# Where zero products go on TensorE: placed by a running shortfall of array activity, and into a free PSUM bank too

## The chip, the cores and the metric

The kernel runs on one core of one Trainium2 chip. The metric is device time in microseconds (us) of one execution. The core's engines run side by side, each through its own list of instructions in order, and wait for one another on semaphores: TensorE (PE) for matmuls, ScalarE (ACT) for exponentials and gelus, VectorE (DVE) for copies out of PSUM, norms and arithmetic, GpSimd (POOL) for small odd jobs, and SyncE (SP), which issues DMAs. PSUM, where matmuls write, has eight banks of 128 x 512 numbers in f32.

## The reference

The input x has 2048 rows of 512. Two kinds of layer alternate, A, B, A, B, with the same weights both times, and each adds its output to x. Layer A is attention with 32 heads of width 16 that share one key and one value head; layer B is a mixer along the rows followed by an MLP.

```python
def _A_ref(x, wq, wk, wv, wo):          # x is layernorm(x); H = 32, Dh = 16
    q = (x @ wq).reshape(B, S, H, Dh).transpose(0, 2, 1, 3)
    k = x @ wk
    v = x @ wv
    p = _softmax(jnp.einsum("bhqd,bkd->bhqk", q, k) * (Dh ** -0.5))
    o = jnp.einsum("bhqk,bkd->bhqd", p, v)
    return o.transpose(0, 2, 1, 3).reshape(B, S, H * Dh) @ wo

def _B_ref(x, w1, w2, w3, w4):          # w3: 512 x 1792, w4: 1792 x 512
    h = _gelu(_layernorm(x) @ w1)
    # four column groups of h are shifted by 1, -1, 2, -2 rows: hs
    x1 = x + hs @ w2
    return x1 + _gelu(_layernorm(x1) @ w3) @ w4
```

The exponentials are most of the elementwise work: 2 x 32 x 2048 x 2048 of them.

## The kernel before

**Tiling.** The queries are cut into four chunks c of 512 rows, the heads into eight blocks b of four, the keys into 16 blocks kb of 128. One *group* is (layer, c, b, kb): four score matmuls (one for each head, line 730), each on a quarter of the array's rows (32*128), into four banks; four exponentials; and four value matmuls (line 824), each on a quarter of the array's columns (128*32), that add into the accumulator bank ACC (bank 5). There are 1024 groups. After the 16 groups of a block (`block_end`, lines 833 to 884) a DVE copy takes ACC out (line 849, or its siblings 837 and 845 where a block of the second layer is spilled and added later); reciprocals and small matmuls (lines 856 to 877) then divide by the softmax sums.

**Who computes the exponentials.** Score banks 0 to 2 and 3 to 4 are two slots that alternate. A *unit* (`declare_unit`, line 750) is one slot's score matmuls and one ACT exponential over its two or three banks (line 775). In the three-bank slot the third bank may go to DVE instead, which computes the exponential by integer arithmetic (lines 790 to 812). `assign` (line 930) gives DVE a pair of tiles when its backlog is short.

**Side work.** When a chunk's attention is done, `chunk_end` (line 951) declares all that follows for its rows: output projection (993), mixer (1027, 1069), MLP (1102, 1133), norms and transposes (582), and the next keys, values and queries (626, 641, 669). This runs beside the attention of later chunks, released at a pace, through the two pool banks 6 and 7. A side operation takes a free pool bank when it is placed and gives it back when its reader has ended (`Late`, `take`, `give`). The long gelus on ACT (lines 1041 and 1119) interrupt the exponentials. After the last attention unit the attention's banks are lent to the pool and the tail runs alone.

**The planner.** The order of each engine's instructions is made while the program is built, by `Plan`, which plays the run through with costs of its own. `_pick` takes from an engine's ready operations the one with the lowest priority number: 0 for score units, 2 for value groups, 4 to 10 for side work. `soon` in `_pick` keeps everything with a priority above 0 back while a score unit will be ready within 0.2 us. The planner models the TensorE clock: it counts full-array columns (`activity`) in windows of 3.4133 us, and a window with at least `WARM` x 2400 columns per us makes the next one run at 2400 columns per us, otherwise at 1200. On the chip only the order and the semaphores remain; no planned time is enforced.

**Fillers.** To keep activity up, the planner places zero products: a 128 x 128 block of zeros (NIL) times ONES, added into ACC, where it changes nothing (line 743). `debt` is the shortfall: `KEEP` x 2400 columns per us of time, less the columns placed, and never under -`CREDIT` (0.3 us). In the kernel before, a filler is asked for only when `_pick` found nothing at all for PE and `idle()` (line 139) says yes: a shortfall over zero, and no attention operation ready within `NEAR_FILL` (0.25 us). It has priority 20. `filler()` (line 735) places none while the latest block's copy, `last_copy`, has been declared but has not ended, since ACC is then being read. The copy is declared together with the last value group of its block, which is ahead of when it runs.

Of the kernel before, what the change touches and what calls it, by code (L numbers as in the profile page):

```python
# [31 lines left out]
class Plan:  # L32
# [12 lines left out]
    WARM = 0.36  # L45
    KEEP = 0.46
    CREDIT = 0.3
    LATER = 12.0
# [90 lines left out]
    def idle(self):  # L139

        if self.filler is None:
            return False
        t = self.now
        self.roll(t)
        if any(o.prio <= 2 and o.ready <= t + self.NEAR_FILL for o in self.heap["PE"]):
            return False
        return self.debt + self.KEEP * 2400.0 * (t - self.debt_at) > 0

# [56 lines left out]
    def _place(self, o, t):  # L205
# [10 lines left out]
        elif o.eng == "PE":  # L216
# [15 lines left out]
            self.debt = max(self.debt, -self.CREDIT * 2400.0)  # L232
# [19 lines left out]
    def run(self, pump):  # L252
        while True:
# [4 lines left out]
            t = heapq.heappop(self.events)  # L258
# [4 lines left out]
            while again:  # L263
                again = pump(self.now)
                for e in ENGINES:
                    if self.free_at[e] <= self.now + 1e-9:
                        o = self._pick(e, self.now)
                        if o is None and e == "PE" and self.idle():
                            self.filler()
                            o = self._pick(e, self.now)  # L270
                        if o is not None:
                            self._place(o, self.now)
                            again = True
# [85 lines left out]
def mm(n, k=1):  # L359
    return ("F", max(n, 60) * k, n * k)  # L360
# [6 lines left out]
class Kernel:  # L367
# [104 lines left out]
    def head(self):  # L472
# [17 lines left out]
        def fill(eng, ap, v, tags, dur, prio):  # L490
# [5 lines left out]
           reads=[("ID",)], writes=[("ID",)], dur=0.4, prio=-9)  # L496
# [4 lines left out]
           reads=[("ONES",)], pe=mm(512), prio=-9)  # L501
# [233 lines left out]
    def filler(self):  # L735

        dep = self.last_copy
        if dep is not None and not (dep.placed and dep.end + self.pl.MARGIN <= self.pl.now):
            return
        if self.last_fill is not None and not self.last_fill.placed:  # L740
            return
        o = self.last_fill = self.pl.op(
            "PE", lambda e: e.matmul(self.PB[:, self.ACC, :], lhsT=self.NIL, rhs=self.ONES, start=False,  # L743
                                     stop=False, skip_group_check=True),
            reads=[("ONES",)], pe=mm(512), prio=20)
        if dep is not None:
            o.preds.add(dep)
        self.nfill += 1
# [436 lines left out]
```

## Time and profile before

| | us |
|---|---|
| median of 3 runs | 1913.28 |
| lowest and highest | 1908.33 and 1926.69 |
| the profiled execution's own time | 1905.72 |
| its span, first to last instruction | 1903.9 |
| PE busy in it | 1764.9 (93%) |
| DVE busy | 1648.0 (87%) |
| ACT busy | 1683.7 (88%) |
| mean granted TensorE clock | 0.855 |
| fillers (line 743) | 547 |

How to read it: the page gives busy time for each engine, then the span in 40 slices with the busy share in tenths, and under PEclk the TensorE clock that the throttle granted, in tenths of full speed. Its groups name a line, an engine, an operation, the tiles out<-in, the shape, and the count, then busy time and mean ns, then the engine's idle time before them and who ended it. The trace also answers for any stretch of time (`from:to`): length, then the busy time and the number of instructions of each engine, then the granted clock, the DMA share and GB/s. Asked for one line, it gives that line's instructions alone. In order of time a row is: start, duration, engine, line, operation, count of merged instructions, and in brackets the idle time before it and what ended it. Matmuls are pipelined and their ends are modelled, so a row's duration holds some latency; the distance between two starts is the better measure of what one occupies.

### The profile page before, as it was taken

To read this page: it belongs to the slowest core of one execution; us is meant where nothing else is said; L and a number is where in the kernel's file an instruction comes from. 1 tells how busy PE (TensorE), PEld (TensorE's weight loads), DVE (VectorE), ACT (ScalarE), POOL (GpSimd) and SP (SyncE) were. 2 spreads that over 40 slices of the span, in tenths; PEclk is the share of its full clock that TensorE was granted. 3 is DMA by queue.
4 is the path that set the end of the run, shared out by engine and by line. 5 is a ranking of instruction groups with operands and counts; after the bars stand their busy time and mean duration, and the time that the engine had idled before them with its cause. 6 is when DMAs were issued, how large, how long until landed. Compare 5 with 4: busy or idle time off the path is not lost.

```text
span 1903.9 us, 32587 instructions
## 1 busy us (share of the span) xinstructions
PE 1764.9 (93%) x13284; PEld 509.4 (27%) x13284; DVE 1648.0 (87%) x3209; ACT 1683.7 (88%) x1726; POOL 59.6 (3%) x117
## 2 busy tenths in 40 slices
PE   8999999999999899999889899999899998989988
PEld 3222222323222222223222222222222222222234
DVE  7988899998889999997989589878888998999942
ACT  5999999999999999996899689888988999999942
POOL 2000000000100000001000000000000000000000
PEclk9855587999799997999989779587887989995989
DMA  5000000000000000000000000000000000000000
GB/s 167 1 1 1 1 1 1 1 1 1 1 1 1 1 1 1 1 1 1 1 1 1 1 1 1 1 1 1 1 7 4 1 1 7 7 1 1 1 12 14
DMA packets 10179, 12.07 MB, mean 6 GB/s; under 512 B 1584, under 2 KB 9520, under 8 KB 10032
## 3 DMA queue, kind: packets, MB, share of 16 engines
q1 hardware_dynamic: 10032, 10.00, 1.7%
q8 instruction: 106, 1.74, 0.4%
q14 instruction: 41, 0.34, 0.1%
HBM read 7.90 MB, written 2.10 MB: 5 GB/s over the span
## 4 chain that ended last, share of the span: by engine, by line
PE 54%; ACT 36%; DVE 9%; issue 1%; DMA 0%; POOL 0%; SPq 0%
ACT EA L775 33%; PE PB L730 20%; PE PB L824 12%; PE PB L1133 5%; PE PB L743 4%; PE PB L993 3%; PE PB L1102 3%; DVE DJ L790 2%; PE PB L669 2%; ACT G L1119 2%; PE PB L1027 1%; PE PB L582 1%; DVE ED L810 1%; DVE ED L812 1%; PE PB L1069 1%; PE PB L871 1%
## 5 line engine op out<-in xcount | busy, mean ns | idle before, releaser
L775 ACT ACTIVATE EA<-PB 128x1024 bf16<-128x1024 f32 (+2 forms) x1639 | 1571.9, 1063 | 158.2 <-PE PB L730 142.3
L730 PE MATMUL PB<-QT,KT 32*128 32x512 bf16 x4096 | 738.4, 444 | 92.9 <-ACT EA L775 70.9
L790 DVE TENSOR_SCALAR DJ<-PB 128x512 uint16<-128x512 f32 x768 | 527.9, 687 | 116.2 <-PE PB L730 111.6
L824 PE MATMUL PB<-EA,VP 128*32 128x512 bf16 x3328 | 460.0, 449 | 3.9 <-ACT EA L775 3.4
L730 PEld LDWEIGHTS PB<-QT,KT 32*128 32x128 bf16 x4096 | 161.1, 93 | 667.9 <-ACT EA L775 515.2
L824 PE MATMUL PB<-ED,VP 128*32 128x512 bf16 x768 | 339.6, 450 | 0.0
L810 DVE TENSOR_TENSOR ED<-DF,ED 128x1024 bf16<-128x1024 uint16 x384 | 261.9, 682 | 2.6
L812 DVE TENSOR_TENSOR ED<-DJ,ED 128x1024 uint16<-128x1024 uint16 x384 | 262.4, 683 | 1.1
L743 PE MATMUL PB<-ONES,NIL 128*128 128x512 bf16 x547 | 185.4, 414 | 0.7 <-DVE ACCF L849 0.7
L824 PEld LDWEIGHTS PB<-EA,VP 128*32 128x32 bf16 x3328 | 102.0, 95 | 303.2 <-issue 262.0
L804 DVE TENSOR_SCALAR DF<-DJ 128x1024 uint16<-128x1024 uint16 x384 | 162.1, 422 | 3.4
L807 DVE TENSOR_SCALAR ED<-DF 128x1024 bf16<-128x1024 uint16 x384 | 161.5, 421 | 3.6
L1133 PE MATMUL PB<-W,G 128*128 128x512 bf16 x448 | 129.2, 408 | 14.0 <-ACT G L1119 13.4
L1102 PE MATMUL PB<-ZT,W 128*128 128x384 bf16 (+2 forms) x560 | 134.2, 354 | 0.9 <-DVE ZT L589 0.7
L669 PE MATMUL PB<-YT,WQ 128*32 128x512 bf16 x1024 | 77.7, 405 | 3.1 <-DVE QT L676 1.8
L993 PE MATMUL PB<-WO,OT 128*128 128x512 bf16 x256 | 72.3, 391 | 0.7 <-DVE OT L877 0.7
L743 PEld LDWEIGHTS PB<-ONES,NIL 128*128 128x128 bf16 x547 | 47.7, 100 | 94.3 <-issue 75.7
L1112 DVE CAST G<-PB 128x512 bf16<-128x512 f32 (+2 forms) x112 | 67.6, 604 | 4.2 <-PE PB L1102 4.1
L824 PEld LDWEIGHTS PB<-ED,VP 128*32 128x32 bf16 x768 | 70.7, 95 | 0.0
L558 POOL TENSOR_SCALAR SM<-MV 128x4 f32<-128x4 f32 (+3 forms) x29 | 8.5, 293 | 1569.3 <-DVE MV L543 1569.2
L1102 PEld LDWEIGHTS PB<-ZT,W 128*128 128x128 bf16 x560 | 42.3, 99 | 55.2 <-issue 32.5
L849 DVE CAST ACCF<-PB 128x512 bf16<-128x512 f32 x57 | 39.1, 686 | 19.5 <-PE PB L824 19.0
(80 smaller groups left out, 902.3 us busy)
## 6 DMA issues: line engine op xcount, KB each, us to landing
W<-in_B_w_dram SPq DMA_DIRECT2D x2, 1792.0 KB, 12.7
X<-in_A_x_dram SPq DMA_DIRECT2D x8, 256.0 KB, 6.5
out_dram<-OUTB SPq DMA_DIRECT2D x16, 128.0 KB, 1.7
W<-in_B_w_dram SPq DMA_DIRECT2D x2, 512.0 KB, 6.7
WQ<-in_A_wq_dram SPq DMA_DIRECT2D x1, 512.0 KB, 5.9
WO<-in_A_wo_dram SPq DMA_DIRECT2D x4, 128.0 KB, 2.8
WK<-in_A_wk_dram SPq DMA_DIRECT2D x1, 16.0 KB, 6.7
WV<-in_A_wv_dram SPq DMA_DIRECT2D x1, 16.0 KB, 6.1
```

The lines of the kernel that those rows point to most:

```text
L730: return e.matmul(self.PB[:, bank, :], lhsT=self.KT[32 * h:32 * h + 32, la, kb * 128:(kb + 1) * 128], rhs=self.QT[32 * h:32 * h + 32, c % ...
L743: "PE", lambda e: e.matmul(self.PB[:, self.ACC, :], lhsT=self.NIL, rhs=self.ONES, start=False, stop=False, skip_group_check=True),
L775: o = op("ACT", lambda e: e.activation(self.EA[:, ea, 0:n, :], self.PB[:, b0:b0 + n, :], ACTF.Exp, scale=0.25), writes=[("BK", b) for b in ...
L790: o = op("DVE", lambda e: e.tensor_scalar(out=self.DJ[:, js, i * 512:(i + 1) * 512], in0=self.PB[:, bank, :], scalar1=128 * LOG2E * 0.25, ...
L804: op("DVE", lambda e: e.tensor_scalar(out=self.DF, in0=J, scalar1=0x7F, scalar2=None, op0=ALU.bitwise_and), reads=jt, writes=[("DF",)], du ...
L807: op("DVE", lambda e: e.tensor_scalar(out=E, in0=self.DF, scalar1=-129.0, scalar2=0.33 / 128, op0=ALU.add, op1=ALU.mult), reads=[("DF",)], ...
L810: op("DVE", lambda e: e.tensor_tensor(out=E, in0=self.DF, in1=E, op=ALU.mult), reads=[("DF",)], writes=et, dur=t_x2(1024), prio=2, side=Fa ...
L812: last = op("DVE", lambda e: e.tensor_tensor(out=E.bitcast(dt.uint16), in0=J, in1=E, op=ALU.add), reads=jt, writes=et, dur=t_x2(1024), pri ...
L824: ins = e.matmul(self.PB[32 * h:32 * h + 32, self.ACC, :], lhsT=self.VP[:, la, kb, :], rhs=e4[h][0], start=first, stop=(end is not None), ...
L993: ins = e.matmul(self.PB[:, L.bank, :], lhsT=self.OT[:, b, q:q + 128], rhs=self.WO[:, b, :], start=(b == 0), stop=(b == 7))
L1102: ins = e.matmul(self.PB[:, L.bank, 0:n], lhsT=self.W3[:, dc, f * 128:(f + 1) * 128], rhs=ZT[:, dc, 0:n], start=(dc == 0), stop=(dc == 3))
L1133: ins = e.matmul(self.PB[:, L.bank, :], lhsT=self.G2[:, f, i * 128:(i + 1) * 128], rhs=self.W4[:, f, :], start=(f == 0), stop=False)
```

## The change

Fillers are now considered before anything else is picked for PE. If the shortfall is over `FORCE` (0.3 us) a filler is placed even if attention is ready; if it is over zero, one is placed unless attention is ready within a look-ahead, which is `NEAR_FILL` (0.25 us) for a shortfall under `URGENT` (0.4 us) and 0 otherwise. Its priority is -20, ahead of all other work. The shortfall is held under `CAP` (0.65 us). `KEEP` goes from 0.46 to 0.53, `WARM` in the clock's model from 0.36 to 0.40. While ACC may not be touched, a filler may take a free pool bank, which it writes as a product of its own (start and stop set) and gives back at once. The first dummy matmul into ACC gets priority -30 and a tag that fillers wait for.

```diff
-    WARM = 0.36
-    KEEP = 0.46
+    WARM = 0.40
+    KEEP = 0.53
     CREDIT = 0.3
+    URGENT = 0.4
+    FORCE = 0.3
+    CAP = 0.65
...
         t = self.now
         self.roll(t)
-        if any(o.prio <= 2 and o.ready <= t + self.NEAR_FILL for o in self.heap["PE"]):
+        short = (self.debt + self.KEEP * 2400.0 * (t - self.debt_at)) / 2400.0
+        if short <= 0:
             return False
-        return self.debt + self.KEEP * 2400.0 * (t - self.debt_at) > 0
+        if short > self.FORCE:
+            return True
+        near = self.NEAR_FILL if short < self.URGENT else 0.0
+        return not any(o.prio <= 2 and o.ready <= t + near for o in self.heap["PE"])
...
-            self.debt = max(self.debt, -self.CREDIT * 2400.0)
+            self.debt = min(max(self.debt, -self.CREDIT * 2400.0), self.CAP * 2400.0)
...
+                        if e == "PE" and self.idle():
+                            self.filler()
                         o = self._pick(e, self.now)
-                        if o is None and e == "PE" and self.idle():
-                            self.filler()
-                            o = self._pick(e, self.now)
...
-           reads=[("ONES",)], pe=mm(512), prio=-9)
+           reads=[("ONES",)], writes=[("ACC0",)], pe=mm(512), prio=-30)
...
     def filler(self):
 
-        dep = self.last_copy
-        if dep is not None and not (dep.placed and dep.end + self.pl.MARGIN <= self.pl.now):
-            return
         if self.last_fill is not None and not self.last_fill.placed:
             return
+        dep = self.last_copy
+        L = None
+        if dep is not None and not (dep.placed and dep.end + self.pl.MARGIN <= self.pl.now):
+            if not any(t + self.pl.MARGIN <= self.pl.now for t, b in self.pl.pool):
+                return
+            L = Late()
         o = self.last_fill = self.pl.op(
-            "PE", lambda e: e.matmul(self.PB[:, self.ACC, :], lhsT=self.NIL, rhs=self.ONES, start=False,
-                                     stop=False, skip_group_check=True),
-            reads=[("ONES",)], pe=mm(512), prio=20)
-        if dep is not None:
+            "PE", lambda e: e.matmul(self.PB[:, self.ACC if L is None else L.bank, :], lhsT=self.NIL,
+                                     rhs=self.ONES, start=L is not None, stop=L is not None, skip_group_check=True),
+            reads=[("ONES",), ("ACC0",)], pe=mm(512), prio=-20, take=L, give=L)
+        if dep is not None and L is None:
             o.preds.add(dep)
```

## The prediction

> **What bounds the kernel now.** I read the page first.
>
> ```profile
> span 1903.9 us, 32587 instructions
> ...
> PE 1764.9 (93%) x13284; PEld 509.4 (27%) x13284; DVE 1648.0 (87%) x3209; ACT 1683.7 (88%) x1726; POOL 59.6 (3%) x117
> ...
> PEclk9855587999799997999989779587887989995989
> ...
> PE 54%; ACT 36%; DVE 9%; issue 1%; DMA 0%; POOL 0%; SPq 0%
> ...
> L775 ACT ACTIVATE EA<-PB 128x1024 bf16<-128x1024 f32 (+2 forms) x1639 | 1571.9, 1063 | 158.2 <-PE PB L730 142.3
> ...
> L730 PE MATMUL PB<-QT,KT 32*128 32x512 bf16 x4096 | 738.4, 444 | 92.9 <-ACT EA L775 70.9
> ...
> L743 PE MATMUL PB<-ONES,NIL 128*128 128x512 bf16 x547 | 185.4, 414 | 0.7 <-DVE ACCF L849 0.7
> ```
>
> ScalarE (ACT) works 1683.7 of 1903.9 us, nearly all of it in the exponentials of line 775. Of its idle time, 142.3 us ends when score matmuls of line 730 finish, so TensorE is what it waits for. TensorE has two clocks: the PEclk line dips to 5. The zero products of line 743, which I call fillers, are there 547 times. Reading the granted clock along the span, I found where it switches between 1.00 and 0.50 and asked for the busy times of stretches cut there: first the ten half-clock stretches that will turn out to begin at a block's end, then 15 full-clock ones of the main loops.
>
> ```profile
> core 0: us, PE busy (x) PEld busy (x) DVE busy (x) ACT busy (x) POOL busy (x), PEclk, DMA share, GB/s
> 77.80:251.90 174.10, 171.80 (x1017) 35.24 (x1013) 153.84 (x277) 166.84 (x170) 0.00 (x0) 0.50 0.00 1
> ...
> 1716.20:1764.00 47.80, 47.21 (x288) 10.43 (x288) 44.02 (x82) 43.37 (x46) 0.94 (x3) 0.50 0.00 1
> sum 416.40, PE 411.49 PEld 92.52 DVE 354.78 ACT 368.67 POOL 0.94; mean PE 41.15 PEld 9.25 DVE 35.48 ACT 36.87 POOL 0.09
> ```
>
> ```profile
> 306.50:497.70 191.20, 186.47 (x1516) 56.41 (x1512) 180.82 (x357) 189.23 (x197) 6.60 (x11) 1.00 0.01 1
> ...
> sum 1025.10, PE 945.48 PEld 279.63 DVE 976.88 ACT 1001.17 POOL 33.32; mean PE 63.03 PEld 18.64 DVE 65.13 ACT 66.75 POOL 2.22
> ```
>
> The next sums are, in this order, five half-clock stretches that follow a long gelu, two others, and the rest (head, change of layer, tail).
>
> ```profile
> sum 64.90, PE 59.66 PEld 11.41 DVE 37.80 ACT 47.98 POOL 0.19; mean PE 11.93 PEld 2.28 DVE 7.56 ACT 9.60 POOL 0.04
> sum 47.80, PE 46.92 PEld 10.04 DVE 37.01 ACT 38.40 POOL 0.00; mean PE 23.46 PEld 5.02 DVE 18.50 ACT 19.20 POOL 0.00
> sum 349.70, PE 301.37 PEld 115.77 DVE 241.57 ACT 227.48 POOL 25.20; mean PE 75.34 PEld 28.94 DVE 60.39 ACT 56.87 POOL 6.30
> ```
>
> At full clock ACT idles 23.9 of 1025.1 us, 2.3%. At half clock it idles 47.7 of 416.4, 16.9 of 64.9 and 9.4 of 47.8: 14% of 529 us. The other 122.2 us of idle lie in the head, the layer change and the tail, where one stage waits for the one before.
>
> What switches the clock? I cut one stretch into windows of 3.4 us, first with all matmuls, then (last two rows) with the fillers alone.
>
> ```profile
> 71.00:74.40 3.40, 2.91 (x21) 0.70 (x19) 3.19 (x7) 3.40 (x5) 0.00 (x0) 1.00 0.03 5
> 74.40:77.80 3.40, 2.36 (x22) 0.69 (x22) 3.26 (x7) 3.40 (x6) 0.00 (x0) 1.00 0.00 0
> 77.80:81.20 3.40, 2.93 (x19) 0.53 (x15) 3.40 (x7) 3.40 (x5) 0.00 (x0) 0.50 0.00 0
> 98.30:101.70 3.40, 3.40 (x19) 0.63 (x16) 2.57 (x5) 3.21 (x4) 0.00 (x0) 0.50 0.00 0
> ...
> 71.00:74.40 3.40, 1.00 (x3) 0.21 (x3) 1.00 0.03 5
> 98.30:101.70 3.40, 0.61 (x1) 0.11 (x1) 0.50 0.00 0
> ```
>
> A score (32*128) or value (128*32) matmul uses a quarter of the array for 512 columns, a filler all of it; at 2400 columns per us a window takes 8160. From 71.0 on: (18/4 + 3) x 512 = 3840, a share of 0.47, and the clock stays full. From 74.4 on: 22/4 x 512 = 2816, 0.345, and the next window is at half. At 98.3 PE is busy all the time, yet (18/4 + 1) x 512 gives 0.345 and nothing recovers. I did this for all 525 windows between 20 and 1812 us. Of 370 full-clock windows, the 336 at 0.40 or more are all followed by full clock, the 15 under 0.355 never, of the 19 between 17. Of 155 half-clock ones, none of the 82 under 0.32 is, 5 of 37 from 0.32 to 0.355, 7 of 31 from 0.355 to 0.40, 5 of 5 above. So the clock follows the amount of array work, and the limit lies near 0.37.
>
> Why the work runs out shows at the ten entries: first the copies of line 849 from 1 us before to 3 us after an entry, then the fillers in the 3.4 us before it.
>
> ```profile
> 76.80:80.80 4.00, 0.68 (x1) 0.63 0.00 0
> ...
> 1715.20:1719.20 4.00, 0.68 (x1) 0.63 0.01 2
> ...
> 74.40:77.80 3.40, 0.00 (x0) 0.00 (x0) 1.00 0.00 0
> ...
> sum 34.00, PE 0.67 PEld 0.07; mean PE 0.07 PEld 0.01
> ```
>
> Nine of the ten rows hold one such copy; the tenth entry (1118.9) has its sibling of line 845. Fillers: 0.67 us in 34. That is the rule in the old filler(): from the moment a block's copy is declared until it has ended, no filler may enter the accumulator bank. The kernel loses the clock there, and once at half it stays, since attention alone lies under the limit.
>
> **The change, part by part.** *The free pool bank* takes that gap away. If all ten stretches ran at ACT's full-clock share, 368.67 / 0.977 = 377.4 us would replace 416.4: 39 us. I take 35, since about one stretch in ten may stay. The largest is worth little: in its 174 us ACT idles only 7.3. With the 16 and 9 us of the other two sums (below) all half-clock time of the main loops is worth 63 us, 3.3% of the span. [...]
>
> *Running shortfall, KEEP 0.53, forcing.* How a filler fits shows in order of time, two ACT steps at full clock and one at half:
>
> ```profile
> 68.10 0.39 PE L730 MATMUL PB<-QT,KT 32*128 32x512 bf16 x3 [0.20 <-ACT EA L775]
> 68.42 0.40 PE L824 MATMUL PB<-EA,VP 128*32 128x512 bf16 x3
> 68.43 0.39 PE L824 MATMUL PB<-ED,VP 128*32 128x512 bf16 x1
> 69.02 0.39 PE L730 MATMUL PB<-QT,KT 32*128 32x512 bf16 x2 [0.20 <-ACT EA L775]
> 69.34 0.60 PE L743 MATMUL PB<-ONES,NIL 128*128 128x512 bf16 x2
> 69.93 0.39 PE L730 MATMUL PB<-QT,KT 32*128 32x512 bf16 x3
> ...
> 79.10 0.61 PE L730 MATMUL PB<-QT,KT 32*128 32x512 bf16 x3 [0.31 <-ACT EA L775]
> 79.64 0.61 PE L824 MATMUL PB<-EA,VP 128*32 128x512 bf16 x3
> ```
>
> At full clock three steps last 3 x 0.92 = 2.75 us and hold three score units, two value groups and two fillers. From start to start a unit takes 0.32 us; a second filler behind the first adds 0.60 - 0.39 = 0.21, so a change of kind costs about 0.11. Occupied: 5 x 0.32 + 0.53 = 2.13 of 2.75 us. Work: (16/4 + 2) x 512 = 3072 of 6600 columns, 0.465, which is the old KEEP. For 0.53 it takes 2.8 fillers, 0.8 more, which at 0.32 each need 0.26 of the 0.62 us that are free. So at full clock there is room.
>
> How many more: over all pairs of such windows from 77.8 to 1812.9 us I took today's fillers out and filled up to 0.53. That needs 872, an estimate, where the same stretch now holds 514: about 360 more. What does one cost? At least 0 where it fills a hole, at most 0.32 us where a score unit stands behind it: 0 to 115 us. A gain from them is the clock, which is counted above. The nearest rows are two stretches at full clock with many and with few fillers (first all, then fillers alone):
>
> ```profile
> 400.00:450.00 50.00, 48.93 (x352) 15.41 (x349) 42.56 (x83) 49.75 (x51) 0.00 (x0) 1.00 0.00 1
> 600.00:650.00 50.00, 44.35 (x368) 13.00 (x364) 49.78 (x97) 49.77 (x55) 0.00 (x0) 1.00 0.00 1
> ...
> 400.00:450.00 50.00, 15.39 (x56) 4.88 (x56) 1.00 0.00 1
> 600.00:650.00 50.00, 5.05 (x13) 1.24 (x13) 1.00 0.00 1
> ```
>
> With 56 fillers ACT works 49.75 of 50 us, with 13 it works 49.77: no price at all. Those stood behind the guard that looks 0.25 us ahead for attention. It stays for a shortfall up to 0.3 and is gone above, where a filler is forced. (FORCE is 0.3 and URGENT 0.4, so the branch that would drop the look-ahead to 0 is never reached.) So what the rows don't show is a forced filler ahead of a ready score unit. A filler now has priority -20 too and stands ahead of side work. I take 0.03 us, a tenth of the upper end, near the row: 11 us. The cover is ACT's 0.92 us step; where PE has no hole in it, the upper end holds.
>
> *CAP 0.65* keeps a long shortfall from being paid in one burst. Such bursts stand in the gelus, where ACT is busy for two windows:
>
> ```profile
> 1361.20:1364.70 3.50, 0.61 (x2) 0.11 (x2) 0.91 (x2) 3.48 (x3) 0.00 (x0) 0.99 0.00 0
> ...
> 1357.80:1361.20 3.40, 1.69 (x7) 0.60 (x7) 1.00 0.01 2
> ```
>
> Seven fillers run at once, then PE does two matmuls in 3.5 us, and the clock falls. On the chip nothing spaces fillers in time; they run as soon as their turn comes. So the cap cures this in part: of the 64.9 - 47.98/0.977 = 15.8 us that these five stretches could give I take 8; of the 47.8 - 38.40/0.977 = 8.5 us of the two others, 4.
>
> *At no cost*: a filler that borrows bank 6 or 7 holds it for its own 0.39 us and delays side work that wants it. Around a block's end in sparse attention there is little; without that cover, 71 block ends (64 blocks and 7 spills) x 0.39 = 28 us. The first dummy matmul's priority and its new write tag change an order before any attention. WARM 0.40 only makes the planner expect half clock a little earlier, and lies above the measured limit. No wait on another engine is added: a filler in a pool bank follows that bank's last reader, which the planner has seen end 0.2 us before. The queues of SP and POOL aren't touched.
>
> Sum: 1905.7 (the profiled execution's own time, 1.8 over its span) - 35 - 8 - 4 + 11 = 1870. That execution is 7.6 us below the median of the three runs shown, 1913.28, and just below the lowest, 1908.33. The same ratio on the median gives 1877; I give 1873. What is late next is ACT itself.
>
> **Rivals.** *The price eats the gain.* The forced filler goes ahead of a score unit that is ready, and ACT starts late. It needs 47/360 = 0.13 us per filler, four tenths of the upper end. For it: line 730's 70.9 us of waits on ACT show that scores start the moment ACT lets go of a bank. Against it: the 0.62 us free in three steps. Time about 1905, within 1%. Chance 0.12.
>
> *Half clock with fillers (slower).* The fillers' places come from the planner's clock, not the chip's. Where the chip is at half while the plan thinks it full, a unit takes 79.64 - 79.10 = 0.54 us, and three steps with 2.8 fillers need 5 x 0.54 + 0.54 + 1.8 x (2 x 0.21) = 4.0 us in place of 2.75: 0.46 us lost per us of ACT's time, where today's stretch loses nearly nothing. The share would be (4 + 2.8) x 512 / (4.0 x 2400) = 0.36, from which 7 in 31 windows recover, so such a stretch lasts some 4 windows. If x of the 529 us stay cold, 63 x (1 - x/529) is won and 11 + 0.46 x lost: it decides from x = 90 us on. With a third left (176 us) the time is 1905.7 - 42 + 81 + 11 = 1956. For it: the gelu rows, where the chip and the plan part. Against it: the ten entries that go away hold 416 of the 529 us. Chance 0.15.
>
> *The gate looks at idle gaps.* If gaps set the clock and not the amount of work, more fillers could not lift it, since attention leaves no gap of a window's length with or without them; they would only cost their 11 us: 1917. Against it: from 77.8 to 251.9 PE is busy 171.80 of 174.10 us at clock 0.50, and the windows sort by work. Chance 0.03. [...]
>
> **How the numbers follow.** Forecast (faster, 1842 to 1893) 0.70, price 0.12, half clock 0.15, gaps 0.03. The forecast's bounds are 1842 (all 63 us, fillers free) and 1893 (0.10 us per filler). The range 1838 to 1918 takes in the price and the gaps and leaves out the half-clock case and a little below. One per cent, about what a measurement of this kernel can tell from no change, is 19 us: faster 0.70, same 0.15, slower 0.15.
>
> **What would show it.** Right: a mean granted clock over 0.95 (now 0.855); the stretch 78 to 252 us at full clock; no half-clock entry with a copy of line 849 beside it; some 900 matmuls of line 743; ACT's idle time in line 775 down by about 40 us, its busy time as now. The price rival: a high clock, but line 775's wait for line 730 at 142 us or more. The slower rival: long stretches at 0.5 with several fillers per 3.4 us and ACT under 75% busy. Wrong from the start would be a filler count near 547.

## The result and the profile after

The changed kernel takes 1830.97 us (median of 4 runs, 1823.81 to 1838.65). Four runs of the kernel before, beside them, have a median of 1910.80. The ratio is 0.9607, with a 95% interval of 0.9533 to 0.9680: faster by 3.9%. All ratios in this document, this one included, compare fast runs alone (here with means of 1831.1 and 1906.1 us), a run counting as slow when it is over 1.5% above the fastest of its kernel in its set. The forecast said faster, but 1873 us, with 1838 as the low end. The profiled execution took 1828.43 us, 77.3 less than the 1905.72 of before; the forecast for this difference was 36.

Lines of the new line numbers: 737 are the score matmuls (730 before), 785 the exponentials on ACT (775), 753 the fillers (743), 834 the value matmuls (824), 859 the copy of a block's accumulator (849).

From the page of the changed kernel, the lines that answer to those of before:

```profile
span 1826.6 us, 33349 instructions
...
PE 1668.0 (91%) x13557; PEld 531.9 (29%) x13770; DVE 1646.2 (90%) x3227; ACT 1656.1 (91%) x1724; POOL 62.6 (3%) x117
...
PEclk9999999996999999999999999999999999999999
...
ACT 50%; PE 36%; DVE 12%; issue 1%; POOL 0%; DMA 0%; SPq 0%
...
L785 ACT ACTIVATE EA<-PB 128x1024 bf16<-128x1024 f32 (+2 forms) x1639 | 1546.9, 1082 | 109.8 <-PE PB L737 99.8
...
L753 PE MATMUL PB<-ONES,NIL 128*128 128x512 bf16 x896 | 294.2, 393 | 7.5 <-issue 5.4
...
L753 PEld LDWEIGHTS PB<-ONES,NIL 128*128 128x128 bf16 x1033 | 84.4, 98 | 169.3 <-issue 145.8
```

The clock line dips once, in the tenth slice; the mean granted clock is 0.986, before it was 0.855. The chain of waits has changed sides: PE carried 54% of it and ACT 36%, now ACT 50% and PE 36%. There are 1033 fillers, counted by their weight loads (some of the matmul records are missing from this trace), 486 more than before.

Where did the 77.3 us go? ACT's idle time fell from 1903.9 - 1683.7 = 220.2 us to 1826.6 - 1656.1 = 170.5, by 49.7. Its *busy* time fell too, by 27.6 us, for nearly the same work. There are 1639 exponentials on either side, but 45 of them span three banks where 51 did, and two table loads of 1.28 us are gone; that is some 5 us of the 27.6, an estimate from the mean times of these instructions. The two sums make up the 77.3.

The same by stage. I cut both spans at the ends of the same blocks: the head with block 0; blocks 1 to 8; 9 to 32; 33 to 46; 47 to 70 (seven of these 71 ends are spills); the tail. A row holds the length, ACT's busy time and instructions, the clock, DMA share and GB/s. Before:

```profile
55.40:262.30 206.90, 199.00 (x205) 0.58 0.00 1
262.30:917.20 654.90, 615.48 (x629) 0.93 0.00 1
917.20:1149.10 231.90, 197.85 (x199) 0.87 0.00 1
1149.10:1829.70 680.60, 624.09 (x634) 0.84 0.01 2
```

After:

```profile
53.50:242.70 189.20, 187.85 (x205) 1.00 0.00 1
242.70:911.30 668.60, 614.26 (x630) 0.97 0.00 1
911.30:1131.20 219.90, 196.37 (x199) 0.99 0.00 1
1131.20:1747.90 616.70, 603.78 (x630) 0.99 0.01 3
```

Blocks 1 to 8 gain 17.7 us: 6.6 of idle time and 11.1 of busy time, with 205 instructions in both rows. Blocks 33 to 46 gain 12.0 and the last stage 63.9 (some 8 of that is an MLP gelu that has moved into the tail, where 4.5 are lost). Blocks 9 to 32 *lose* 13.7: they hold the one new half-clock stretch, which the dip in the clock line shows.

Why does an engine become less busy with the same work? In order of time, an unbroken stream of exponentials and one that starts behind a gap (changed kernel; start, duration, and in brackets the idle time before it and what ended it):

```profile
94.25 11.24 ACT L785 ACTIVATE EA<-PB 128x1024 bf16<-128x1024 f32 x12
...
413.92 1.02 ACT L785 ACTIVATE EA<-PB 128x1024 bf16<-128x1024 f32 x1 [0.51 <-PE PB L737]
```

Twelve in a row take 0.94 us each, one that had to wait takes 1.02: in a stream the record of an instruction overlaps the one before it (in the changed kernel at full clock a record of 1.08 us, the mean, adds 0.92), behind a gap it doesn't. Counted over both traces, an exponential of 128x1024 right behind another adds 0.92 us to ACT's busy time and one behind a gap 1.02, at full clock and at half clock alike (0.92 to 0.93 in the stream). Before, 371 stood behind a gap, now 170 do; at 0.10 us each the 201 fewer are 21 us, which with the 5 us above explains nearly all of the 27.6. The page shows the same: 1639 x 1.082 us is 1773, but line 785 was busy 1546.9, so 226 us are overlap; before, 1639 x 1.063 - 1571.9 left 170. So in these two traces a starved ACT looks busier than a fed one (1683.7 us against 1656.1), and each small wait costs some 0.10 us more than the idle time that is booked for it.

### The profile page after: what moved, and what is told of

Read it like the earlier page. It is cut to its first block, busy times and chain, and to the rows that moved or that the text cites. A ratio compares the mean times of both kernels' runs of the same rounds, so it can differ in the third digit from the quotient of the medians.

```text
span 1826.6 us, 33349 instructions
## 1 busy us (share of the span) xinstructions
PE 1668.0 (91%) x13557; PEld 531.9 (29%) x13770; DVE 1646.2 (90%) x3227; ACT 1656.1 (91%) x1724; POOL 62.6 (3%) x117
## 4 chain that ended last, share of the span: by engine, by line
ACT 50%; PE 36%; DVE 12%; issue 1%; POOL 0%; DMA 0%; SPq 0%
ACT EA L785 46%; PE PB L737 11%; PE PB L834 6%; PE PB L1143 5%; PE PB L1112 3%; DVE DJ L800 3%; PE PB L753 3%; PE PB L1003 3%; ACT G L1129 2%; DVE ED L820 1%; DVE ED L822 1%; PE PB L1037 1%; PE PB L1079 1%; ACT L785 1%; DVE ED L817 1%
## 5 line engine op out<-in xcount | busy, mean ns | idle before, releaser
L785 ACT ACTIVATE EA<-PB 128x1024 bf16<-128x1024 f32 (+2 forms) x1639 | 1546.9, 1082 | 109.8 <-PE PB L737 99.8
L737 PE MATMUL PB<-QT,KT 32*128 32x512 bf16 x4096 | 652.7, 387 | 113.9 <-ACT EA L785 84.6
L834 PE MATMUL PB<-EA,VP 128*32 128x512 bf16 x3322 | 402.3, 392 | 4.1 <-ACT EA L785 2.1
L753 PE MATMUL PB<-ONES,NIL 128*128 128x512 bf16 x896 | 294.2, 393 | 7.5 <-issue 5.4
L834 PE MATMUL PB<-ED,VP 128*32 128x512 bf16 x774 | 297.5, 392 | 0.0
L753 PEld LDWEIGHTS PB<-ONES,NIL 128*128 128x128 bf16 x1033 | 84.4, 98 | 169.3 <-issue 145.8
L1112 PE MATMUL PB<-ZT,W 128*128 128x384 bf16 (+2 forms) x542 | 123.2, 342 | 2.7 <-issue 1.9
L1143 PE MATMUL PB<-W,G 128*128 128x512 bf16 x422 | 118.8, 393 | 4.7 <-issue 2.4
L1003 PE MATMUL PB<-WO,OT 128*128 128x512 bf16 x242 | 65.0, 382 | 3.1 <-issue 1.4
L1143 PEld LDWEIGHTS PB<-W,G 128*128 128x128 bf16 x448 | 34.6, 98 | 52.8 <-issue 26.4
```

Source lines behind the costliest of these rows:

```text
L737: return e.matmul(self.PB[:, bank, :], lhsT=self.KT[32 * h:32 * h + 32, la, kb * 128:(kb + 1) * 128], rhs=self.QT[32 * h:32 * h + 32, c % ...
L753: "PE", lambda e: e.matmul(self.PB[:, self.ACC if L is None else L.bank, :], lhsT=self.NIL, rhs=self.ONES, start=L is not None, stop=L is ...
L785: o = op("ACT", lambda e: e.activation(self.EA[:, ea, 0:n, :], self.PB[:, b0:b0 + n, :], ACTF.Exp, scale=0.25), writes=[("BK", b) for b in ...
L834: ins = e.matmul(self.PB[32 * h:32 * h + 32, self.ACC, :], lhsT=self.VP[:, la, kb, :], rhs=e4[h][0], start=first, stop=(end is not None), ...
L1003: ins = e.matmul(self.PB[:, L.bank, :], lhsT=self.OT[:, b, q:q + 128], rhs=self.WO[:, b, :], start=(b == 0), stop=(b == 7))
L1112: ins = e.matmul(self.PB[:, L.bank, 0:n], lhsT=self.W3[:, dc, f * 128:(f + 1) * 128], rhs=ZT[:, dc, 0:n], start=(dc == 0), stop=(dc == 3))
```

## The experiments

Twelve kernels ran, four at a time, each four with runs of the kernel before on the same chip: its medians there were 1925.50, 1924.21 and 1928.39 us. The means that the ratios below are taken against are some 1920, 1899 and 1915 us, so the ratios of the second four (thin fillers, each filler twice, without forcing, fillers inside a gelu) come out some 1% higher than those of the others. With 2% as the least difference that counts, the old level in the changed kernel is faster than the kernel before, all but the pool bank and the level alone are the same, and the other nine are unclear; their ratios are sizes with an interval, not verdicts. The changed kernel's own 0.9607 is from another measurement, so between it and an experiment I compare times, and take nothing under 1% as a difference.

**The pool bank alone**, in the kernel before: the old constants, the old guard, priority 20, and a filler may take a free pool bank while ACC is closed.

```diff
         dep = self.last_copy
-        if dep is not None and not (dep.placed and dep.end + self.pl.MARGIN <= self.pl.now):
-            return
+        L = None
+        if dep is not None and not (dep.placed and dep.end + self.pl.MARGIN <= self.pl.now):
+            if not any(t + self.pl.MARGIN <= self.pl.now for t, b in self.pl.pool):
+                return
+            L = Late()
...
-            reads=[("ONES",)], pe=mm(512), prio=20)
+            reads=[("ONES",)], pe=mm(512), prio=20, take=L, give=L)
```

> The kernel before with one part of the change alone: while a block's copy is pending, a filler may take a free pool bank; constants, guard and priority as before. Theory 1 (the clock is lost where fillers were barred at a block's end): the ten half-clock entries beside block copies go away, and with them most of the gain: ratio 0.965 to 0.975 to the kernel before, mean granted clock over 0.95. Rival (0.46 without forcing lets the work dip under the limit anyway, and the barred stretch was only where it showed): ratio 0.985 to 1.0, half-clock entries elsewhere, clock under 0.92.

Measured: 1874.35 us, ratio 0.9773 [0.9685, 0.9862], clock 0.935, 603 fillers. It lies between the two expectations. The place where it works is as foreseen. Here are blocks 3 to 7 of the first chunk, in which nothing but attention runs: first this kernel's exponentials, then its fillers.

```profile
101.00:219.20 118.20, 117.72 (x130) 1.00 0.00 1
...
101.00:219.20 118.20, 31.44 (x87) 7.23 (x87) 1.00 0.00 1
```

The same five blocks, exponentials alone, take 131.00 us in the kernel before and 118.30 in the changed one:

```profile
104.20:235.20 131.00, 126.22 (x129) 0.50 0.00 1
```

```profile
99.50:217.80 118.30, 117.68 (x130) 1.00 0.00 1
```

So in attention without side work the bank alone does all that the whole change does, with 17 fillers per block. A block costs 2.5 us more at half clock, 11%, and only part of that shows as idle time. What the bank leaves are half-clock stretches in the later chunks, beside gelus and side work. All engines of this kernel in three of them, and their sum:

```profile
726.00:763.50 37.50, 37.34 (x199) 8.09 (x200) 24.43 (x49) 26.51 (x26) 1.67 (x2) 0.50 0.00 1
...
1330.00:1364.00 34.00, 33.77 (x182) 6.48 (x182) 25.37 (x46) 28.99 (x31) 0.00 (x0) 0.50 0.01 5
sum 108.90, PE 108.51 PEld 21.92 DVE 73.63 ACT 83.22 POOL 1.67; mean PE 36.17 PEld 7.31 DVE 24.54 ACT 27.74 POOL 0.56
```

ACT works 76% of these 109 us. Stretches like these are what the rest of the change has left to take away. By the two ratios a little over half of the gain is the bank's (2.3 of 3.9%); that is a rough share, from two measurements, and the parts don't simply add up, as the next runs show.

**All but the pool bank**: the changed kernel, in which a filler finds ACC closed and returns, as it used to.

```diff
         if dep is not None and not (dep.placed and dep.end + self.pl.MARGIN <= self.pl.now):
-            if not any(t + self.pl.MARGIN <= self.pl.now for t, b in self.pl.pool):
-                return
-            L = Late()
+            return
```

> The changed kernel without the pool bank: fillers are barred at a block's end again, but the shortfall is forced before and after it and KEEP is 0.53. Theory 1: entries beside block copies come back, ratio 0.98 to 1.0 to the kernel before. Rival (forcing and KEEP carry the gain): ratio 0.96 to 0.97, as the whole change. A cold stretch with many fillers should last longer or cost more than the ones before if the slower rival of the prediction is real: 0.46 us lost per us of ACT's time.

Measured: 1933.63 us, 1.0067 [1.0028, 1.0106], with 1071 fillers and a clock of 0.948. No gain, rather a loss, at a clock that is higher than that of the bank alone. Half-clock stretches beside copies are back, as expected, but most are short: 198 us at half clock in all, where the kernel before has 553. The chip is mostly at full clock and still nothing is won. In order of time around a block's end (its copy runs at 100.7), PE and then ACT of this kernel:

```profile
101.25 0.39 PE L737 MATMUL PB<-QT,KT 32*128 32x512 bf16 x2 [0.51 <-ACT EA L783]
101.57 3.20 PE L751 MATMUL PB<-ONES,NIL 128*128 128x512 bf16 x14
104.69 0.60 PE L737 MATMUL PB<-QT,KT 32*128 32x512 bf16 x5
```

```profile
94.49 8.54 ACT L783 ACTIVATE EA<-PB 128x1024 bf16<-128x1024 f32 x9
105.13 4.69 ACT L783 ACTIVATE EA<-PB 128x1024 bf16<-128x1024 f32 x5 [2.11 <-PE PB L737]
```

Fourteen fillers stand in a row ahead of a score unit that is ready, and ACT waits 2.11 us. Such runs, 6 to 18 fillers long, follow many of the copies. My explanation: the planner, kept from placing fillers at the block's end, thinks that its clock has fallen to 1200 columns per us. A filler then takes it 512/1200 = 0.427 us, in which 0.53 x 2400 x 0.427 = 543 new columns fall due: each forced filler leaves the shortfall larger than it found it. A later experiment tests this.

**The level alone**, in the kernel before.

```diff
-    WARM = 0.36
-    KEEP = 0.46
+    WARM = 0.40
+    KEEP = 0.53
```

> The kernel before with the two constants alone, KEEP 0.53 and WARM 0.40. Theory 1: the bar at a block's end stays, so its entries stay: ratio 0.985 to 1.0, clock 0.85 to 0.90. Rival (a higher level carries the windows over the barred stretch): ratio under 0.975.

Measured: 1896.62 us, 0.9875 [0.9811, 0.9938], clock 0.856, 804 fillers. 257 more fillers, and the clock of the profiled execution is where it was; ratio and clock are within the first expectation. The longest half-clock stretch of before is still there (all engines):

```profile
74.90:252.40 177.50, 175.16 (x1035) 35.85 (x1031) 156.77 (x283) 170.32 (x174) 0.00 (x0) 0.50 0.00 1
```

The gate of the block's end isn't opened by asking for more. Its 1% goes mostly with the clock all the same: its four runs have clocks of 0.856 to 0.868, the thirteen of the kernel before beside them 0.831 to 0.858. At like clocks the times differ by some 4 to 9 us (1899.68 us at 0.856 and 1898.18 at 0.859, against 1908.43 at 0.855 and 1902.35 at 0.858). Why its clock is a little higher stays open.

**The old level in the changed kernel.**

```diff
-    WARM = 0.40
-    KEEP = 0.53
+    WARM = 0.36
+    KEEP = 0.46
```

> The changed kernel with the old constants, KEEP 0.46 and WARM 0.36; pool bank, forcing, cap and priority stay. Theory 1: no entries beside block copies, ratio within 0.01 of the whole change (0.96 to 0.97), with some 200 fillers fewer. Rival (the level is what matters): ratio 0.98 or more, with windows between 0.30 and 0.37 of array work at the entries.

Measured: 1860.57 us, 0.9698 [0.9636, 0.9760], clock 0.966, 786 fillers. The ratio is within the first expectation. Some 30 us above the changed kernel, with ACT's idle time before line 785 at 139.9 us against 109.8: the higher level would be worth between one and two per cent, though the intervals of the two ratios overlap.

**Thin fillers.** The same order of instructions on every engine as in the changed kernel, but each zero product streams 32 columns in place of 512.

```diff
-            "PE", lambda e: e.matmul(self.PB[:, self.ACC if L is None else L.bank, :], lhsT=self.NIL,
-                                     rhs=self.ONES, start=L is not None, stop=L is not None, skip_group_check=True),
+            "PE", lambda e: e.matmul(self.PB[:, self.ACC if L is None else L.bank, 0:32], lhsT=self.NIL,
+                                     rhs=self.ONES[:, 0:32], start=L is not None, stop=L is not None, skip_group_check=True),
```

> The changed kernel with each filler cut from 512 to 32 columns: every instruction, wait and place stays, only the fillers' array work goes (to a sixteenth). If the clock follows the amount of array work, sparse attention falls to half clock: mean granted clock 0.65 to 0.85, time 1880 to 1960 us. If the clock follows idle gaps, or the gain comes from the new order and not from the clock, nothing gets slower: clock over 0.95 and 1815 to 1835 us.

Measured: 2061.82 us, 1.0859 [1.0778, 1.0940], clock 0.723. From its page, and then its exponentials in the five blocks of the first chunk:

```profile
PE 1908.2 (93%) x13770; PEld 550.4 (27%) x13770; DVE 1672.9 (81%) x3227; ACT 1707.1 (83%) x1724; POOL 63.6 (3%) x117
...
PEclk9655657868587895667777955766677687975599
...
L785 ACT ACTIVATE EA<-PB 128x1024 bf16<-128x1024 f32 (+2 forms) x1639 | 1597.8, 1042 | 293.5 <-PE PB L737 271.6
```

```profile
103.10:235.10 132.00, 124.59 (x129) 0.50 0.00 1
```

The time is past the 1880 to 1960 us expected, on the expected side. This settles one thing for this kernel: the clock follows the amount of array work. PE is busy for longer here than in any kernel so far (1908 us; its share, 93%, is above the changed kernel's 91%), every engine has the same instructions in the same order, and the clock is lost (0.723 against 0.986). No idle gap does it: the first long half-clock stretch begins at 64.4 us, and in the two windows before it PE never idles for over 0.4 us. It also shows what the new order is worth by itself in these five blocks, where both kernels are at half clock: 132.00 us against 131.00 before, so nothing. That the order brings nothing in the rest of the span either is likely, since the whole is 8.6% slower than before, but not shown, since the clock is lower too. The overlap of ACT's records shrinks to 1639 x 1.042 - 1597.8 = 110 us, which continues the scale of 226 and 170. ACT's busy time is 1707.1 us here and 1656.1 in the changed kernel, with exactly the same 1724 instructions.

**Each filler twice.**

```diff
+        def two(e):
+            for _ in range(2):
+                ins = e.matmul(self.PB[:, self.ACC if L is None else L.bank, :], lhsT=self.NIL, rhs=self.ONES,
+                               start=L is not None, stop=L is not None, skip_group_check=True)
+            return ins
...
...
+            "PE", two,
```

> The changed kernel with each filler issued twice, in the same place: some 1030 more matmuls of 512 columns, 0.21 us each behind their twin, 217 us of TensorE in all, at full clock. It measures the price of a filler by itself. Prediction's price of 0.03 us per filler: 31 us more than the changed kernel, ratio to the kernel before 0.975 to 0.98. Fillers for free: within 8 us of the changed kernel, ratio 0.96 to 0.965. Prediction's price rival (0.13 us or more): 130 us more, ratio over 1.02. The clock should be at 0.98 or higher in all three.

Measured: 1940.99 us, 1.0221 [1.0144, 1.0297], at a clock of 0.998: 110 us above the changed kernel for 1033 more fillers, 0.107 us each, between the expectation's 0.03 and 0.13. A line of its page; then all engines in the five blocks, and the fillers alone:

```profile
PE 1890.8 (97%) x14803; PEld 598.8 (31%) x14803; DVE 1662.7 (86%) x3227; ACT 1694.4 (87%) x1724; POOL 62.2 (3%) x117
...
107.30:241.30 134.00, 134.00 (x994) 38.57 (x991) 115.84 (x208) 124.66 (x129) 0.00 (x0) 1.00 0.00 1
...
107.30:241.30 134.00, 71.49 (x252) 16.53 (x252) 1.00 0.00 1
```

PE has no hole left. At full clock these blocks now take longer than at half clock before (131.00). ACT again has the same 1724 instructions and is busy 1694.4 us where the changed kernel has 1656.1, though the clock is full: as in the two traces above, it is the waiting for scores that makes ACT's busy time grow (in the five blocks ACT idles 9.3 of 134.00 us, in the changed kernel 0.6 of 118.30), and half clock is one way to cause it.

**Without forcing**: fillers still come first and the shortfall still runs, but above 0.3 us it isn't ahead of ready attention.

```diff
-        if short > self.FORCE:
-            return True
         near = self.NEAR_FILL if short < self.URGENT else 0.0
```

> The changed kernel without the forced branch: a filler is placed only where no attention is ready within the look-ahead (0.25 us, or 0 where the shortfall is over 0.4). Forcing matters: half-clock entries return, clock under 0.95, ratio 0.975 to 0.99. Forcing doesn't matter (there are holes enough): within 0.005 of the changed kernel.

Measured: 1960.41 us, 1.0321 [1.0207, 1.0436], clock 0.924, though it has 1140 fillers, more than the changed kernel. Two of its half-clock stretches, all engines:

```profile
630.60:715.90 85.30, 85.30 (x405) 17.30 (x404) 65.96 (x115) 75.18 (x74) 0.00 (x0) 0.50 0.00 1
828.60:883.20 54.60, 54.56 (x262) 10.89 (x259) 36.09 (x63) 50.65 (x49) 0.00 (x0) 0.50 0.00 1
```

That is slower than either expectation. Forcing isn't a detail: without it the stretches beside side work last some 50 to 85 us, and one block at the change of layer takes 93.5 us where the changed kernel needs 38.8. Side work came late there; why, I can't say. Half clock can't be the whole cause, since this kernel has 297 us of it and is slower than the kernel before, which has 553. This kernel can also reach the branch that drops the look-ahead to 0, so two things differ.

**Fillers inside a gelu**: the changed kernel, in which a filler is also placed when nothing else is ready and ACT is planned busy for over 1.2 us more.

```diff
                         o = self._pick(e, self.now)
+                        if o is None and e == "PE" and self.filler is not None \
+                                and self.free_at["ACT"] > self.now + 1.2:
+                            self.filler()
+                            o = self._pick(e, self.now)
```

> The changed kernel, and beside it a filler whenever the planner finds nothing else for TensorE and ACT is planned to be busy for over 1.2 us more, which is in the long gelus. In the changed kernel's profile its one long half-clock stretch (410 to 441 us) follows a gelu in which 14 fillers ran at once and TensorE then idled 4.2 us; the blocks there took 15 us longer than in the kernel before. If that is the cause, no half-clock stretch over 7 us is left between 20 and 1740 us and the time falls by 8 to 15 us, to 1816 to 1823 us (ratio 0.952 to 0.957). If not, the time is within 5 us of the changed kernel and half-clock entries stay.

It was aimed at the one new half-clock stretch. In the changed kernel, PE in order of time, then windows of all engines:

```profile
404.26 3.18 PE L753 MATMUL PB<-ONES,NIL 128*128 128x512 bf16 x14 [0.16 <-issue]
411.64 0.61 PE L737 MATMUL PB<-QT,KT 32*128 32x512 bf16 x3 [4.19 <-ACT EA L785]
```

```profile
403.50:406.90 3.40, 3.24 (x20) 1.44 (x19) 3.37 (x7) 3.39 (x3) 0.00 (x0) 1.00 0.00 0
406.90:410.30 3.40, 0.55 (x3) 0.05 (x1) 0.22 (x1) 3.38 (x3) 0.00 (x0) 1.00 0.00 0
410.30:441.10 30.80, 28.80 (x122) 5.17 (x124) 16.52 (x29) 18.96 (x20) 0.00 (x0) 0.50 0.00 1
```

ACT is in a gelu; the fillers that were planned through it run at once, 14 in 3.18 us, and PE stands idle for the next 4.19. The window with 3 matmuls is followed by 30.8 us at half clock with ACT busy 62%. Measured with the edit: 1835.18 us, 0.9662 [0.9567, 0.9757], clock 0.987, 1065 fillers. No net gain: that stretch goes away, another one (378.9 to 396.0) comes. The expectation missed.

**The runs behind the copies, tested**: all but the pool bank, as in the second experiment, but the planner always counts with full clock.

```diff
-            f = 2400.0 if self.warm else 1200.0
+            f = 2400.0
```

> The kernel without the pool bank (ratio 1.0067), with one line more: the planner always counts TensorE at full clock. In that kernel's profile runs of 6 to 18 fillers stand 1 to 2.6 us behind block copies, and ACT idles 2 to 5 us beside each. Theory: after the barred stretch the planner expects half clock, where 512 columns take 0.427 us and 0.53 x 2400 x 0.427 = 543 fall due, so the shortfall never sinks and each next filler is forced, until the planned window is warm. With the planned clock full a filler pays 512 against 272, so runs behind copies are at most 3 long: ACT's idle time there goes, ratio 0.97 to 0.985. Rival (the runs are the capped shortfall of 0.65 us paid back, not the planned clock): runs as long as before, ratio 1.0 to 1.01.

Measured: 1899.26 us, 0.9891 [0.9753, 1.0029], clock 0.941, 889 fillers. The long runs behind copies with ACT idle are gone (those that are left lie in gelus with ACT busy), and ACT's idle time before the exponentials falls from 189.5 us to 152.8. So the runs come from the planned half clock, as worked out above. The gain is smaller than expected, and against the kernel before it isn't clear of noise; the clock still falls at the block ends (222 us at half clock).

**The changed kernel with that same edit.**

```diff
-            f = 2400.0 if self.warm else 1200.0
+            f = 2400.0
```

> The changed kernel with the planner always at full clock. Its own profile has only two runs of 7 to 9 fillers with ACT idle beside them (2.0 and 3.7 us) outside the layer change. Theory: little to win, the time within 8 us of the changed kernel (ratio 0.957 to 0.965). Rival (the forced runs get the chip out of half clock, so they are worth their price): half-clock stretches last longer, mean clock under 0.97, and 10 us or more are lost.

Measured: 1851.35 us, 0.9671 [0.9574, 0.9768], clock 0.976, 1001 fillers: 20 us more than the changed kernel, the loss that the rival named, at a clock a little above its 0.97. A half-clock stretch from 1003 to 1030 us is new. With the pool bank, a planner that knows of half clock seems to be of use (by 20 us, while the intervals of the two ratios overlap); without it, it did harm.

**Every second filler twice.**

```diff
+        times = 1 + self.nfill % 2
+
+        def some(e):
+            for _ in range(times):
+                ins = e.matmul(self.PB[:, self.ACC if L is None else L.bank, :], lhsT=self.NIL, rhs=self.ONES,
+                               start=L is not None, stop=L is not None, skip_group_check=True)
+            return ins
```

> The changed kernel with every second filler issued twice: some 516 more matmuls of 512 columns at the same places, half of what doubling all of them added (1033 for 110 us, 0.107 us each). If each filler has the same price, 55 us more than the changed kernel, 1886 us. If the price comes in only when the holes are full, clearly less than half: under 35 us more, under 1866 us.

Measured: 1856.18 us, 0.9692 [0.9598, 0.9787], clock 0.997: 25 us more than the changed kernel for 516 more fillers, 0.05 each, which is the second expectation. Its fillers in the five blocks, and then those of the changed kernel (the second number in brackets counts the weight loads, which are complete):

```profile
100.60:222.40 121.80, 53.54 (x173) 13.22 (x191) 1.00 0.00 1
```

```profile
99.50:217.80 118.30, 38.90 (x111) 10.01 (x127) 1.00 0.00 1
```

With the rows above this is a curve, at full clock in the same five blocks: 118.2 us with 87 fillers, 118.3 with 127, 121.8 with 191, 134.0 with 252. An additional filler costs nothing, then 3.5/64 = 0.055 us, then 12.2/61 = 0.20. The 87 were placed by the old rule and the others by the new one, and the doubled ones are not spaced by the planner, so the curve is a rough measure and not a law; for stretches with side work there is none.

**Both, the gelu rule and the full-clock plan.**

```diff
+                        if o is None and e == "PE" and self.filler is not None \
+                                and self.free_at["ACT"] > self.now + 1.2:
+                            self.filler()
+                            o = self._pick(e, self.now)
...
-            f = 2400.0 if self.warm else 1200.0
+            f = 2400.0
```

> The changed kernel with both: fillers in ACT's long gelus wherever nothing else is ready, and the planner always at full clock. With the gelus filled alone the time was 1835 us, no gain. If what is left is set by half-clock stretches, 1815 to 1825 us; if by work on ACT and DVE and by the change of layer, within 8 us of the changed kernel.

Measured: 1839.23 us, 0.9608 [0.9478, 0.9739], clock 0.982; 8 us above the changed kernel, with 65 us at half clock. No version has a lower median than the changed kernel. Holding the shortfall under CAP, and the priority of -20, were not tried alone.

## Why the prediction was right, and where it was wrong

**The mechanism was right.** Of what would show it: the clock is over 0.95 (0.986); the stretch from 78 to 252 us is at full clock; no half-clock entry has a block copy beside it; there are 1033 fillers where "some 900" was said; ACT's idle time fell, by 49.7 us where the gross gain in the sum was 35 + 8 + 4 = 47. That these two lie so near is in part luck: the 49.7 holds a loss of 14.9 us in blocks 9 to 32 and a gain of 43.6 in the last stage alone. Room for 2.8 fillers in three steps of ACT: the five blocks hold 127 in 130 steps, 2.9.

**The step that failed is the price of half clock, "all half-clock time of the main loops is worth 63 us".** The mechanism stood; this term was too small. The sum divided ACT's busy time in the half-clock stretches by its busy share at full clock, and so took the busy time for fixed work ("its busy time as now"). It fell by 27.6 us, some 21 of which are the 201 exponentials that no longer start behind a gap; some 5 have to do with neither clock nor gaps, but with the three-bank units and table loads. The thin and the doubled fillers show the same the other way round: the same ACT instructions, busy 51 and 38 us longer. "The largest is worth little: in its 174 us ACT idles only 7.3" came to 3.3 us in that working; blocks 1 to 8, which hold that stretch, gained 17.7. The prediction's own rows could have shown half of it: 174.10 us with 170 ACT instructions is 1.024 us each, 191.20 with 197 is 0.971. Counting the work done per us, and not the share of busy time, gives 170 x 0.053 = 9 us for this stretch. The changed kernel does 0.910 in the five blocks.

**The price, "0.03 us" for each of 360 fillers, 11 us, seems too high.** At this level it is nothing that the five blocks can show; the row that I leaned on (56 fillers, "no price at all") was the better answer. What the fillers cost in stretches with side work no run shows by itself. The bound of 0.32 us held in the runs: the dearest fillers of the curve cost 0.20 us each, where PE's holes are full (busy 134.00 of 134.00 us). One bound was added up wrong: with 0.10 us for each of 360 fillers the sum gives 1905.7 - 47 + 36 = 1895 and not 1893, which changes nothing here.

**The gelus.** That "the cap cures this in part", 8 us of 15.8, was right in the mechanism (bursts of fillers that nothing spaces in time: 14 in 3.18 us in the changed kernel), and the changed kernel has one such stretch of its own, which costs blocks 15 and 16 some 15 us by their ends. Most of the stretches at gelus went away all the same: half clock in the main loops fell from 529 us to some 44.

Put together: the idle time came as the sum had it, 49.7 for 47; 27.6 us of busy time had been left out; and 11 us of price were charged that don't show. 47 - 11 = 36 was forecast; 36 + 2.7 + 27.6 + 11 = 77.3.

**What was said to cost nothing.** The pool bank's loan: the bank alone made the first chunk as fast as the whole change did, so it costs attention nothing there; no side work runs in that chunk, so what the loan costs side work isn't shown. That URGENT is never reached: right as the code stands. "WARM 0.40 only makes the planner expect half clock a little earlier": too light. What the planner does with an expected half clock seems worth 20 us for the change (full-clock plan, 1851) and stood against it without the pool bank (1934 against 1899). How much of that is WARM itself was not tried. That the parts depend on one another isn't in the sum at all: the bank alone 2.3%, the level alone 1.2%, all but the bank no gain, all together 3.9%.

**The rivals.** *The price eats the gain* needed 0.13 us per filler. At the level of the change the price isn't there. It comes with more fillers: the first 516 more cost 0.05 us each, the next 517 cost 85 us, 0.16 each, and the kernel with every filler doubled has a clock of 0.998 and is 2% slower than before by its ratio. *Half clock with fillers* was a warm plan on a cold chip. What took the gain away without the pool bank is a neighbour of it: a cold plan, on a chip that was mostly warm. Without forcing there are long half-clock stretches again, but with ACT busy 88% and 93% in the two shown, not under the 75% that was to tell this rival, and the cause of that run's time is open. In the changed kernel only some 50 us stayed cold, under the 90 from which it decides. *The gate looks at idle gaps* is refuted by the thin fillers, which keep PE as busy (93% of the span against 91%) and lose the clock (0.723 against 0.986) with no idle time of PE over 0.4 us ahead of it; in the kernel before, the longest in the two windows ahead of the entry at 77.8 us is 0.53. The entry at 410.3 us of the changed kernel, behind 4.19 idle us, would fit this rival; with 3 matmuls in the window before, it fits the amount of work as well.

## What to carry to other kernels

When a lowered clock is to be raised, size the gain by work done per us at the low and at the full clock in stretches of the same kind, not by the idle share of the engine that waits: here the starved engine's busy time grew too (ACT 1707 us with thin fillers and 1656 in the changed kernel, for the same 1724 instructions). In the runs here padding work was free while it filled holes (from 87 to 127 fillers in the five blocks) and dear when they were full (0.20 us each from 191 to 252), so find the level at which it keeps the clock and stop there, and ask first whether anything forbids it at the very place where the clock falls. And test the parts of such a change together, since a rule for how much padding is due can do harm where another rule keeps it from being placed.

## What the runs showed of the hardware that was not expected

In the changed kernel the same exponential is booked with 1.02 us behind a gap and 0.94 (0.905 over five blocks) in a stream, so in these runs ACT's busy total depends on how well it is fed: for the same 1724 instructions it is 1656 us in the changed kernel, 1707 with thin fillers (clock 0.723) and 1694 with doubled ones (clock 0.998). Products of zeros count as activity here: shortening them from 512 columns to 32 takes the clock from 0.986 to 0.723. They seem to count in full: over the 1408 full-clock windows of four traces (before, thin fillers, the bank alone, the level alone) the best limit leaves 20 on the wrong side when a filler counts as 512 full-array columns, and 46 when it counts half. And here the highest clock isn't the lowest time: 0.998 came with 1941 us and 0.986 with 1831.
